# Four edits to a fused attention, gated-MLP and MLP kernel: load order, raw-word buffers, a PSUM bank, and the place of operand splits

## The chip, the cores and the metric

The kernel runs on one core of one Trainium2 chip. The metric is device time in microseconds (us); a measurement is the median of several executions. One execution was also profiled, and all rows below come from it.

## What is computed

Three layers in a row, all in float32, on 3072 tokens (4 sequences of 768) of width 512:

```python
# 1: chunked attention, 8 heads of 64; each chunk of 32 sees 16 keys left, 8 right, 8 memory keys
a = exp(scores - max(scores)); out = (a / sum(a)) @ v_full
# 2: RMS norm, then a gated MLP with 1536 hidden columns
xn = x / sqrt(mean(x * x) + 1e-6) * rms_g
x2 = silu(xn @ w_gate) * (xn @ w_val) @ w_out
# 3: a plain MLP with 2048 hidden columns
h = x2 @ w_in
g = where(h >= 1, h, where(h <= -1, 0, (h + 1) ** 2 / 4))
out = g @ w_out2
```

Weights arrive as float64 and are turned into float32 on the chip. Every product of two float32 matrices is made of three matmuls: each operand is split into a high part (rounded by a copy on ScalarE, ACT) and a low part (a subtraction on VectorE, DVE), and high*high, high*low and low*high are added up in PSUM (`mm3`, L555 to L559).

## The kernel before, in words

**Tiles and stages.** The tokens form six tiles of 512 (`NTT`). Before the first tile, a stretch written out by hand (`ORDER`, L25) runs the attention of the first four units (two units of heads make one pair of 128-row blocks). Then four tiles (t = 0 to 3) go one by one through the gated MLP: for each of 12 hidden blocks f, a gate product, a value product (`proj_in`, L561) and the output product of the block before (`out1`, L583). Each of these three is followed by a `slot` (L736), 36 slots in a tile. A slot holds a piece of the attention for later tiles (`att_slot`, by the tables `plan`, `plan2`, `plan3`) and a piece of weight conversion. The last two tiles go together through the gated MLP as a pair, and then all six tiles, as three pairs, through the last MLP, with a seven-product scheme for 2x2 block matrices (`seven`, L883): seven products of six matmuls instead of eight.

**Order of work.** In tile 0 the order on TensorE (PE) and on the queue of SyncE (SP), which issues most loads, is that of the program text (L674); the other engines are ordered by the compiler. From tile 1 on every engine works in the order of the text (L828). An instruction that must wait holds up all behind it on its engine or queue.

**Raw words.** In tile 0, each slot loads one 512 KB unit of raw float64 words of the gated MLP (`load_w`, L115, 36 units in all) into one of three buffers (`wst`, L72) and converts earlier units: `conv_c` (ACT, L128), `join` (DVE, L138 and L139, which is the last to read the buffer), then the high part (ACT, L152) and the low part (DVE, L154) in `wall`, which PE reads. Units 0 to 2 are loaded in the stretch `ORDER`, one more at each of d0 to d3. The tag `xn` of the pool `xs` holds `v_tail` in that stretch, and later the tile's normalised x; no one uses it in the first slots of tile 0.

**x.** A pair's normalised rows are transposed by PE in two blocks, x0 and x1, in successive slots (`step_x`, L533); four ACT copies take each out of PSUM (`part_X`, L546). Both use the first bank of the two-bank tile `ps_a`, which the attention steps use too. From tile 2 on, x goes to DRAM (L548) and comes back as a 1 MB load `load_x` (L552), which stands ahead of the gate product of f = 9. The next tile's split of x (`split_x`, L350) stands at f = 11. Loads of keys, queries and values (`load_qk`, L376; `load_v`, L392) are issued in the slot whose PE step frees their buffer; `load_v` for the unit after stands in the slot of a `v` step.

**Sevens and blocks ahead.** In `seven`, with five banks A to E, the products p0 to p6 go to A, C, B, A, B, C, B. After p0 and p1, ACT copies A into B (L891), on which p2 goes on adding, and C into `p5` (L892). DVE adds `p5` and B into C (L899) after p2; p4 writes B again, so p4 must wait for L899. After p4 DVE updates `p5` (L903). In the first pair's products `some` (L895) puts steps of weight conversion (`conv_step`) among the products. The hidden values h are used by `Out.run` (L992) in 7 G blocks, each needing a split operand `r`: `split` (L975) is an ACT copy (L982), a DVE subtraction (L984) and, for the first G blocks, a DVE sum written back into h (L986). `ahead(n)` makes the split of block n before the run begins. It stands right behind `proj1(f)` for odd f (L1122) and behind `proj2` for g = 3 to 6 (L1147), so its instructions lie on ACT and DVE ahead of the next seven's copies. `defer` (L893) is a list of calls that a seven makes right behind its two bank copies. At g = 6, the first step of the next pair's x (L812, a 1024-element DVE subtraction) is made behind the splits (L1154).

Of the kernel before, what the change touches and what calls it, by code (L numbers as in the profile page):

```python
# [39 lines left out]
def tile_stream_attention_moe_moe2(  # L40
# [69 lines left out]


    w1 = {}
    raw, absd, f32s = [], [], []

    def load_w(units, n):  # L115
        for _ in range(n):
            if units:
                dst, key, src = units.pop()
                w64 = wst.tile([P, 1024], U32, tag="w64", name="w64")
                nc.sync.dma_start(w64, src)  # L120
                raw.append((dst, key, w64))

# [402 lines left out]
            )  # L525

    def step_x(pr, blk, ps):
        t, o = divmod(pr, 2)
        if t == 1 and t not in xn_t:
            xn_t[t] = xs.tile([P, KK, TT], F32, tag="xn", name="xn")  # L530
        x = x_t[pr]
        for kk in range(KK):
            nc.tensor.transpose(ps[:, 0, kk * P:(kk + 1) * P], x[blk][:, kk * P:(kk + 1) * P], ident)  # L533
        ps_t["x", pr, blk] = ps

    def part_X(pr, blk):
        t, o = divmod(pr, 2)
        ps = ps_t.pop(("x", pr, blk))
        c0 = (2 * o + blk) * P
        if t < 2:  # L540
            xn = xn_t[t][:, :, c0:c0 + P]
        else:
            xn = x_t[pr][blk].rearrange("p (k i) -> p k i", k=KK)
        rows = ps[:, 0, :].rearrange("p (k i) -> p k i", k=KK)
        for kk in range(KK):
            nc.scalar.activation(xn[:, kk], rows[:, kk], AF.Copy, scale=g_t[:, kk:kk + 1])  # L546
        if t >= 2:
            nc.sync.dma_start(x_d[t][:, :, c0:c0 + P], xn)  # L548

    def load_x(t):  # L550
        xn_t[t] = xs.tile([P, KK, TT], F32, tag="xn", name="xn")
        nc.sync.dma_start(xn_t[t], x_d[t])  # L552
# [65 lines left out]
    for st in ORDER.split():  # L618
        c, n = st[0], st[1:]
        if c == "f":  # L620
            fill(slots[free[0]], int(n))
            continue
        n = int(n)
        if c in "savx":
            use[c, n] = free.pop(0)
            ps = slots[use[c, n]]
            if c == "x":
                step_x(n // 2, n % 2, ps)
            else:
                fns[c](n, ps)  # L630
                if n >= 4:
                    done.add(st)
            if c == "s" and n >= 3:
                load_qk(n + 1)
            if c == "v" and n >= 3:
                load_v(n + 1)
            if st == "s0":
                load_qk(3)
                load_v(2)
                load_v(3)  # L640
                load_w(units1, 1)
                nc.sync.dma_start(g_b, rms_g.partition_broadcast(P))
                nc.sync.dma_start(g_t, rms_g.rearrange("(k p) -> p k", p=P))
                load_w(units1, 2)
        elif c == "H":
            if not xhl:
                xh, xl = (xs.tile([P, KK, TT], F32R, tag=tag, name=tag) for tag in ("xh", "xl"))
                xhl.extend((xh[:, kk], xl[:, kk]) for kk in range(KK))
            nc.scalar.activation(xh[:, :, n * P:n * P + P], rows(n), AF.Copy)
        elif c == "L":  # L650
            dst, hi = (x[:, :, n * P:n * P + P] for x in (xl, xh))
            tt_(out=dst, in0=rows(n), in1=hi.bitcast(F32), op=ALU.subtract)  # L652
            free.append(use.pop(("x", n)))
        elif c == "r":
            step_r(n // 2, (n % 2,))
        elif c == "p":
            part_p(n)
        elif c == "c":
            conv_c()
        elif c == "d":  # L660
            conv_d()
            load_w(units1, 1)
        elif c == "g":
            lows.append(conv_hi())
        elif c == "o":
            lows.pop(0)()
        else:
            fns[c](n)
            if c in "mAn":
                free.append(use.pop(({"m": "s", "A": "a", "n": "v"}[c], n)))  # L670
# [31 lines left out]
    def att_step(pr, st):  # L702
        n = int(st[1])
        if st[0] in "sav" and f"{st[0]}{2 * pr + n}" in done:
            return
        if st[0] == "x":
            step_x(pr, n, ps_a)
            part_X(pr, n)
        elif st[0] == "r":
            step_r(pr)  # L710
        else:
            u = 2 * pr + n
            fns[st[0]](u, ps_a)
            for p in parts[st[0]]:
                fn = (lambda p=p: fns[p](u)) if p != "p" else (lambda: part_p(pr) if n else None)
                if pr < 4 or p in "mAn":
                    fn()
                else:
                    (later if p in "kp" else after).append(fn)
        if st[0] == "s":  # L720
            load_qk(2 * pr + n + 1)
        if st[0] == "v":
            load_v(2 * pr + n + 1)
# [101 lines left out]
    for t in range(NS):  # L825
        if t == 1:
            region.close()
            region.enter_context(tc.manual_schedule())  # L828
        for f in range(F1):
            if 0 < t < NS - 1 and f == 9:  # L830
                load_x(t + 1)
            if t == NS - 1 and f == F1 - 1:
                for i in range(8):
                    load_wp(i)
            proj_in(ps_g[0], w1[("g", f)])
            s = sp.tile([P, TT], F32, tag="s", name="s")
            nc.scalar.activation(s, ps_g[0], AF.Silu)
            if t == NS - 1 and f == 8:
                xq.extend(x_steps())
            slot(t, 3 * f)  # L840
            if t == NS - 1 and f == 6:
                att_only.close()
                right = ctx.enter_context(tc.tile_pool(name="right", bufs=1, side="right", reuse_waits="tile"))
                m2["y"] = right.tile([P, 2, KK, TT], F32, name="y")
                load_y(x_d[NS], x_d[NS + 1])
            proj_in(ps_g[1], w1[("v", f)])
            if f == F1 - 1 and t + 1 < NS:
                split_x(xn_t.pop(t + 1))
            nc.vector.tensor_tensor(out=s, in0=s, in1=ps_g[1], op=ALU.mult)
            low = split_h(f, s)  # L850
            if t == 0:
                low()
            slot(t, 3 * f + 1)
            if t:
                low()
            if pend is not None:
                out1(*pend)
            pend = (t, f)
            slot(t, 3 * f + 2)
# [18 lines left out]
        m2["n"] += 1  # L878
        return m2["t"][m2["n"] % len(m2["t"])]

    banks, defer = [], []

    def seven(n, early):  # L883

        A, B, C, D, E = banks
        banks[:] = D, A, E, C, B
        tt = nc.vector.tensor_tensor
        product(7 * n, A, True)
        product(7 * n + 1, C, True)
        p5 = tmp2("p5")  # L890
        nc.scalar.activation(B, A, AF.Copy)  # L891
        nc.scalar.activation(p5, C, AF.Copy)  # L892
        while defer:  # L893
            defer.pop(0)()
        some = lambda k: conv_step(PACE2[n // 4] * k) if n < F1 else None  # L895
        product(7 * n + 2, B, False)
        some(2)
        product(7 * n + 3, A, False)
        tt(out=C, in0=p5, in1=B, op=ALU.add)  # L899
        done11 = early(A)  # L900
        some(2)
        product(7 * n + 4, B, False)
        tt(out=p5, in0=p5, in1=B, op=ALU.add)  # L903
        some(2)
        product(7 * n + 5, C, False)
        some(1)
        product(7 * n + 6, B, False)
        return done11, C, B, p5
# [42 lines left out]
    class Out:  # L951
# [40 lines left out]
        def run(self, A, B, C, extra):  # L992
# [46 lines left out]
            while self.xq:  # L1039
                self.xq.pop(0)()  # L1040

    def done1(j, o, bank, p5):

        for m in range(2):
            d = p5[m] if p5 else tmp2("c")
            if p5:
                tt_(out=d, in0=p5[m], in1=bank[m], op=ALU.add)
            elif (j, o, m) == (1, 0, 1):
                nc.vector.tensor_copy(d, bank[m])
            else:  # L1050
                nc.scalar.activation(d, bank[m], AF.Copy)
            nc.scalar.dma_start(y_d[NS + o][:, 2 * j + m], d)
# [66 lines left out]
    for f in range(F1):  # L1119
        proj1(f)  # L1120
        if f % 2:
            o1.ahead(f // 2 - 1)  # L1122
        if f == 3:
            for i in range(4):
                load_wo(i)
        if f == 5:
            load_y(y_d[0], y_d[1])
            xq.extend(x_steps())
# [13 lines left out]
    for pr in range(NP2):  # L1142
        banks[:] = b3, Y[3], b4, b1, b2
        o2 = Out(G2, n1 + n2 * pr, 4, done2, xq)
        for g in range(G2):
            proj2(G2 * pr + g)
            o2.ahead(g - 3)  # L1147
            if pr and g < 2:
                defer.append(turn(pr - 1, 1, 0, g, Y[g]))
            if g == 3 and pr + 1 < NP2:  # L1150
                load_y(y_d[2 * pr + 2], y_d[2 * pr + 3])
                xq.extend(x_steps())
            if g == 6 and xq:
                xq.pop(0)()  # L1154
        extra = [
            (5 * G2 + 2, lambda: turns(pr, 0, 0)),
            (5 * G2 + 6, lambda: turns(pr, 1, 1)),
# [91 lines left out]
```

## Time and profile before

| what | us |
|---|---|
| three runs: median (lowest, highest) | 1159.44 (1158.72, 1161.72) |
| profiled execution, whole | 1158.09 |
| its span, first to last instruction | 1156.3 |
| busy: PE, DVE, ACT | 1125.6, 820.6, 617.3 |
| mean share of TensorE's clock granted | 0.989 |

The stretches of the span: attention alone until 36 us, tile 0 until 146, tiles 1 to 3 until 504 (tile 2 begins at 272), the first pair's 12 sevens of `proj1` until 619 and its output run until 671; then three times 8 sevens of `proj2` (the first until 755) and an output run, until 1152.

How to read it: PE is busy almost throughout, so the time between the matmuls, and any stretch at a lower clock, is what an edit can change. A row's idle time in square brackets is the engine's wait before that instruction, with what ended it; waits under 0.15 us are not shown there.

### The profile page before, as it was taken

What the parts mean: (1) busy time and instruction counts of PE and PEld (TensorE: products, weight loads), DVE (VectorE), ACT (ScalarE), POOL (GpSimd) and SP (SyncE); (2) the same over time, 40 slices, a digit from 0 to 9 for tenths busy, and PEclk for the clock granted to TensorE, in tenths of its full rate; (3) what the DMA queues carried; (4) which work ended last, traced back from release to release, by engine and by line L of the source; (5) the groups of instructions that cost most, each with busy time, mean ns of one, the idle gap of its engine ahead of it and who ended that gap; (6) DMA issues with size and microseconds to landing.
All of it is one profiled execution on the core that took longest, in us unless ns stands there. A gap on an engine that the chain in (4) does not pass through costs nothing.

```text
span 1156.3 us, 20945 instructions
## 1 busy us (share of the span) xinstructions
PE 1125.6 (97%) x7879; PEld 909.7 (79%) x7879; DVE 820.6 (71%) x1433; ACT 617.3 (53%) x1088; POOL 102.6 (9%) x152
## 2 busy tenths in 40 slices
PE   5899999999999999999999999999999999999998
PEld 4677788877788777887888888788887788887886
DVE  3887667767756666766676867897677887578855
ACT  3777665656565765534444634456444465344553
POOL 0200003213222222101110000000000000000000
PEclk7999999999999999999999999999999999999999
DMA  8776448998979887779997697756778666762564
GB/s 294 253 258 203 163 140 271 312 310 284 303 245 309 269 273 236 275 269 383 404 394 241 213 316 246 210 180 199 231 207 260 177 195 216 217 197 86 164 188 158
DMA packets 144212, 281.81 MB, mean 244 GB/s; under 512 B 15216, under 2 KB 65392, under 8 KB 142320
## 3 DMA queue, kind: packets, MB, share of 16 engines
q1 hardware_dynamic: 123664, 228.57, 60.7%
q0 software_dynamic: 12768, 43.52, 10.8%
q10 hardware_dynamic: 7680, 8.39, 2.1%
q8 instruction: 62, 1.02, 0.3%
q14 instruction: 38, 0.31, 0.1%
HBM read 201.26 MB, written 79.17 MB: 243 GB/s over the span
## 4 chain that ended last, share of the span: by engine, by line
PE 76%; DVE 8%; ACT 6%; DMA 6%; issue 3%; POOL 1%; SPq 0%; DVEq 0%; ACTq 0%; POOLq 0%
PE ps_y L1034 14%; PE ps_g L1034 11%; PE ps_g L557 6%; PE ps_g L559 5%; PE ps_g L558 5%; PE ps_g L872 3%; PE ps_b L872 3%; PE ps_b L874 3%; PE ps_b L873 3%; PE ps_g L874 3%; PE ps_g L873 3%; DMA w<-in_w_dram 3%; PE ps_y L557 3%; PE ps_y L558 3%; PE ps_y L559 3%
## 5 line engine op out<-in xcount | busy, mean ns | idle before, releaser
L557 PE MATMUL ps_g<-xh,wall 128*128 128x512 f32 x384 | 156.6, 408 | 3.2 <-ACT wall L152 3.2
L1034 PE MATMUL ps_y<-r,wo 128*128 128x512 f32 x672 | 156.2, 390 | 0.0
L558 PE MATMUL ps_g<-xl,wall 128*128 128x512 f32 x384 | 151.1, 394 | 0.4 <-DVE xl L652 0.4
L559 PE MATMUL ps_g<-xh,wall 128*128 128x512 f32 x384 | 151.3, 394 | 0.2 <-DVE wall L154 0.2
L1034 PEld LDWEIGHTS ps_y<-r,wo 128*128 128x128 f32 x672 | 125.7, 188 | 26.0
L984 DVE TENSOR_TENSOR r<-h,r 128x512 fp32r<-128x512 f32 x167 | 112.2, 689 | 44.0 <-ACT r L982 43.9
L935 ACT ACTIVATE t<-t,half 128x512 f32<-128x512 f32 x96 | 66.9, 720 | 128.4 <-DVE t L934 125.5
L982 ACT ACTIVATE r<-h 128x512 fp32r<-128x512 f32 x167 | 100.4, 624 | 56.2 <-DVE r L984 18.2
L1034 PE MATMUL ps_g<-r,wo 128*128 128x512 f32 x498 | 116.0, 390 | 0.0
L1034 PEld LDWEIGHTS ps_g<-r,wo 128*128 128x128 f32 x498 | 93.2, 188 | 19.4 <-DVE r L984 0.2
L557 PEld LDWEIGHTS ps_g<-xh,wall 128*128 128x128 f32 x384 | 72.8, 190 | 19.6 <-ACT wall L152 3.8
L559 PEld LDWEIGHTS ps_g<-xh,wall 128*128 128x128 f32 x384 | 72.7, 189 | 17.1 <-DVE wall L154 1.0
L558 PEld LDWEIGHTS ps_g<-xl,wall 128*128 128x128 f32 x384 | 73.0, 190 | 14.3 <-DVE xl L652 0.7
L872 PE MATMUL ps_g<-wall 128*128 128x512 f32 x198 | 78.4, 396 | 1.6 <-DVE ps_y L899 0.8
L872 PE MATMUL ps_b<-wall 128*128 128x512 f32 x202 | 79.2, 392 | 0.7 <-DVE ps_g L899 0.3
L873 PE MATMUL ps_b<-wall 128*128 128x512 f32 x202 | 78.6, 389 | 0.0
L874 PE MATMUL ps_b<-wall 128*128 128x512 f32 x202 | 78.6, 389 | 0.0
L557 PE MATMUL ps_y<-hh,wall 128*128 128x512 f32 x192 | 77.9, 406 | 0.0
L873 PE MATMUL ps_g<-wall 128*128 128x512 f32 x198 | 77.1, 390 | 0.0
L874 PE MATMUL ps_g<-wall 128*128 128x512 f32 x198 | 77.1, 389 | 0.0
L558 PE MATMUL ps_y<-hl,wall 128*128 128x512 f32 x192 | 75.2, 392 | 0.0
L559 PE MATMUL ps_y<-hh,wall 128*128 128x512 f32 x192 | 74.9, 390 | 0.0
(199 smaller groups left out, 2086.7 us busy)
## 6 DMA issues: line engine op xcount, KB each, us to landing
wo<-w2o_d SPq DMA_DIRECT2D x88, 512.0 KB, 3.4
wall<-w2p_d SPq DMA_DIRECT2D x168, 256.0 KB, 2.9
wall<-w1p_d SPq DMA_DIRECT2D x84, 256.0 KB, 5.9
w<-in_w_dram SPq DMA_DIRECT2D x36, 512.0 KB, 4.6
w<-in_w_dram POOLq DMA_DIRECT2D x32, 512.0 KB, 5.7
k_in<-in_k_dram SPq DMA_DIRECT2D x48, 256.0 KB, 4.9
wo<-w1o_d SPq DMA_DIRECT2D x21, 512.0 KB, 3.5
v_in<-in_v_dram SPq DMA_DIRECT2D x40, 260.0 KB, 4.3
```

The lines of the kernel that those rows point to most:

```text
L557: nc.tensor.matmul(ps, wh, xh, start=start, stop=False)
L558: nc.tensor.matmul(ps, wh, xl, start=False, stop=False)
L559: nc.tensor.matmul(ps, wl, xh, start=False, stop=stop)
L872: nc.tensor.matmul(bank, wh, xh, start=st, stop=False, skip_group_check=True)
L873: nc.tensor.matmul(bank, wh, xl, start=False, stop=False, skip_group_check=True)
L874: nc.tensor.matmul(bank, wl, xh, start=False, stop=kk == 1, skip_group_check=True)
L935: nc.scalar.activation(s, s, AF.Square, scale=0.5, bias=half)
L982: nc.scalar.activation(r[:, 0], src, AF.Copy)
L984: tt_(out=r[:, 1], in0=src, in1=r[:, 0].bitcast(F32), op=ALU.subtract)
L1034: nc.tensor.matmul(bank[p][m], a, b, start=s0, stop=s1, skip_group_check=True)
```

## The change

It moves `load_x` behind the slot of f = 9, and so behind what that slot issues. It gives two more raw-word buffers to units 3, 4, 8, 9, 13 and 14, in the memory of the tag `xn`, and loads two units at d0, so that every later unit is popped a slot earlier. It puts x1's transposes in the second bank of `ps_a`. It moves each split ahead of a run, but for the last, into the list `defer`, and the x step of g = 6 into a list `defer2`, which a seven calls behind L899 and the first use of A.

```diff
     def load_w(units, n):
...
                 dst, key, src = units.pop()
-                w64 = wst.tile([P, 1024], U32, tag="w64", name="w64")
+                i = 3 * F1 - 1 - len(units)
+                if i == 3:
+                    spare.append(xs.tile([P, 2, 1024], U32, tag="xn", name="w64s"))
+                if i < 15 and i % 5 > 2:
+                    w64 = spare[0][:, i % 5 - 3]
+                else:
+                    w64 = wst.tile([P, 1024], U32, tag="w64", name="w64")
...
     def step_x(pr, blk, ps):
-            nc.tensor.transpose(ps[:, 0, kk * P:(kk + 1) * P], x[blk][:, kk * P:(kk + 1) * P], ident)
+            nc.tensor.transpose(ps[:, kk * P:(kk + 1) * P], x[blk][:, kk * P:(kk + 1) * P], ident)
...
-        rows = ps[:, 0, :].rearrange("p (k i) -> p k i", k=KK)
+        rows = ps.rearrange("p (k i) -> p k i", k=KK)
...
-                step_x(n // 2, n % 2, ps)
+                step_x(n // 2, n % 2, ps[:, 0])
...
             conv_d()
-            load_w(units1, 1)
+            load_w(units1, 1 if n else 2)
...
-            step_x(pr, n, ps_a)
+            step_x(pr, n, ps_a[:, n])
...
-            if 0 < t < NS - 1 and f == 9:
-                load_x(t + 1)
...
             slot(t, 3 * f)
+            if 0 < t < NS - 1 and f == 9:
+                load_x(t + 1)
...
         done11 = early(A)
+        while defer2:
+            defer2.pop(0)()
         some(2)
...
+    def ahead(o, n, last):
+        if last:
+            o.ahead(n)
+        else:
+            defer.append(lambda: o.ahead(n))
...
         if f % 2:
-            o1.ahead(f // 2 - 1)
+            ahead(o1, f // 2 - 1, f == F1 - 1)
...
-            o2.ahead(g - 3)
+            ahead(o2, g - 3, g == G2 - 1)
...
             if g == 6 and xq:
-                xq.pop(0)()
+                defer2.append(xq.pop(0))
```

## Rows read from the trace of the kernel before

**Rows 1.** The page, its first part: busy us, share, instructions.

```profile
PE 1125.6 (97%) x7879; PEld 909.7 (79%) x7879; DVE 820.6 (71%) x1433; ACT 617.3 (53%) x1088; POOL 102.6 (9%) x152
```

**Rows 2.** Stretches: length, busy PE, PEld, DVE, ACT, POOL, clock, DMA share, GB/s.

```profile
36.00:48.00 12.00, 10.07 (x44) 7.87 (x45) 10.16 (x19) 9.95 (x15) 4.11 (x6) 1.00 0.93 313
60.00:72.00 12.00, 12.00 (x109) 9.30 (x108) 9.66 (x17) 9.67 (x15) 0.00 (x0) 0.86 0.85 288
...
252.00:264.00 12.00, 10.15 (x97) 8.18 (x98) 6.42 (x17) 2.80 (x7) 3.23 (x4) 0.86 0.69 236
```

**Rows 3.** PE's waits, whole span: total us, times, longest.

```profile
PE ps_g L557 <- ACT wall L152: 3.2, 2, 1.6
PE ps_a L453 <- ACT wgv L197: 2.3, 1, 2.3
PE ps_a L453 <- ACT aT L443: 2.2, 4, 0.7
PE ps_a L533 <- ACT x_nat L546: 1.8, 4, 0.6
```

**Rows 4.** Chain that ended last, in tile 0: start, us, what.

```profile
50.29 0.70 DVE tu L139
...
51.06 5.11 DMA w<-in_w_dram
```

**Rows 5.** The same chain in tile 1, around x's load.

```profile
244.96 1.13 SPq L552
...
246.99 7.16 DMA v_in<-in_v_dram
```

**Rows 6.** Timeline of PE in tile 1: start, duration, instruction, idle before.

```profile
253.67 0.35 PE L453 MATMUL ps_a<-v_in,aT 64*32 64x65 f32 x16 [2.35 <-ACT wgv L197]
```

**Rows 7.** Waits of PE's weight loads, 620 to 1157 us.

```profile
PEld ps_g L872 <- ACT ps_g L891: 3.3, 6, 0.5
```

**Rows 8.** Timeline of PE, `proj2`: p1 and p2 for g = 6, p4 for g = 7.

```profile
735.66 0.39 PE L872 MATMUL ps_g<-wall 128*128 128x512 f32 x1
...
737.30 0.50 PE L872 MATMUL ps_b<-wall 128*128 128x512 f32 x1
...
750.62 0.50 PE L872 MATMUL ps_g<-wall 128*128 128x512 f32 x1 [0.38 <-DVE ps_y L899]
```

**Rows 9.** Timeline of ACT in the seven of g = 6.

```profile
736.67 0.58 ACT L891 ACTIVATE ps_b<-ps_g 128x512 f32<-128x512 f32 x1
737.27 0.60 ACT L892 ACTIVATE t<-ps_g 128x512 f32<-128x512 f32 x1
```

**Rows 10.** Timeline of DVE in the sevens of g = 6 and g = 7.

```profile
737.48 0.69 DVE L984 TENSOR_TENSOR r<-h,r 128x512 fp32r<-128x512 f32 x1
738.20 0.69 DVE L986 TENSOR_TENSOR h<-h 128x512 f32<-128x512 f32 x1
739.06 0.70 DVE L899 TENSOR_TENSOR ps_g<-t,ps_b 128x512 f32<-128x512 f32 x1 [0.17 <-PE ps_b L874]
...
748.74 1.22 DVE L812 TENSOR_TENSOR y<-y 128x1024 f32<-128x1024 f32 x1
```

**Rows 11.** Timeline of ACT in the seven of f = 4, `proj1`.

```profile
544.85 0.60 ACT L892 ACTIVATE t<-ps_b 128x512 f32<-128x512 f32 x1 [0.72 <-PE ps_b L874]
```

**Rows 12.** Timeline of DVE in that seven.

```profile
545.39 0.42 DVE L190 TENSOR_TENSOR late<-tu 128x256 f32<-128x256 f32 x1
...
546.06 0.42 DVE L193 TENSOR_TENSOR late<-late,tu 128x256 f32<-128x256 f32 x1
...
546.86 0.69 DVE L899 TENSOR_TENSOR ps_b<-t,ps_y 128x512 f32<-128x512 f32 x1
```

**Rows 13.** Timeline of PE in that seven: the first matmuls of p2, p3, p4.

```profile
544.65 0.39 PE L872 MATMUL ps_y<-wall 128*128 128x512 f32 x1
...
546.01 0.39 PE L872 MATMUL ps_g<-wall 128*128 128x512 f32 x1
...
547.60 0.50 PE L872 MATMUL ps_y<-wall 128*128 128x512 f32 x1
```

More of the change, by code (lines that the diff above doesn't have):

```diff
@@ L112, in tile_stream_attention_moe_moe2 @@
     w1 = {}
-    raw, absd, f32s = [], [], []
+    raw, absd, f32s, spare = [], [], [], []
     def load_w(units, n):
@@ L879, in tmp2 @@
         return m2["t"][m2["n"] % len(m2["t"])]
-    banks, defer = [], []
+    banks, defer, defer2 = [], [], []
     def seven(n, early):
```

## The prediction

> **What bounds the kernel now.** Read the page's busy times first: PE is busy for 97% of the span [rows 1]. So an edit can pay only where PE waits or where its clock is down, and it costs only where it makes PE wait anew. Next come the list of PE's waits [rows 3] and the stretches with a clock under 1.00 [rows 2]; there the reader is to see four places. (1) In tile 0 the value products wait twice for converted weights, 1.6 us each, and the stretch behind the second wait has a mean clock of 0.86. Over 12 us that is 1.7 us of work lost ((1 - 0.86) x 12), which is 3.4 us at the lower level, 1.2 GHz, instead of 2.4. (2) In tile 1 a value step of the attention waits 2.35 us [rows 6], again with 0.86 behind it. (3) x1's transposes wait four times for x0's copies. (4) The weight loads of PE wait for the bank copy L891: six times on one bank [rows 7], three times each on two others, so 12, which are g = 4 to 7 of the three pairs. Last come the timelines of one seven of `proj2` and one of `proj1` [rows 8 to 13], where the reader is to see which instruction stands before which.
>
> Two prices recur. A product of six matmuls takes 1.36 us (p2 to p3, 544.65 to 546.01) [rows 13], 0.23 a matmul; a matmul's row lasts 0.39, so a wait costs PE about 0.16 more than the idle time it shows. And the first matmul behind a wait lasts 0.50 instead of 0.39, another 0.11.
>
> **x load behind attention's loads.** SP issued x's load at 244.96 and the second half of the next unit's values at 246.99; the latter landed 7.16 us later, at 254.15 [rows 5], while PE stood ready at 251.3 (253.67 less 2.35) [rows 6]. Behind the slot, x's 1 MB no longer lies ahead of the values: at the 313 GB/s of a full stretch [rows 2] that is 3.3 us, so they land at about 250.8. PE gets back 2.35 + 0.16 + 1.7 for the clock; I leave 0.2 for a landing that is not quite in time: **-4.0** (bounds -2.4 and -4.4). x's own load now stands on SP also behind the slot's stores of converted sums (L202), which wait for DVE, but x is read two blocks f later; in tile 2 the slot has no value load to free, and the move costs nothing for the same reason. What would uncover it is x landing behind f = 11. The Trainium skill, "DMA: Bandwidth & Descriptors", section "Queues, rings and completion order", says that each DMA engine takes turns between the queue rows that have work, packet by packet. If GpSimd's queue had work all that time, the values' half megabyte would go at half speed and land some 1.7 us later, and this part would be worth about 2.5 less; the one landing here can't tell.
>
> **Two more raw-word buffers.** On the chain in tile 0 a load goes out when a join frees its buffer (50.29) and takes 5.11 us [rows 4]; ACT's conversions wait for it, and PE for them. With five buffers units 3 and 4 go out at once behind `v_tail`'s last reader, and each unit to 14 is two joins ahead. Beyond that a load waits for the same join as before, but stands ahead of the key loads of the slot behind it. No wait for words then remains in slots 0 to 12. Of the first wait (1.6 + 0.16) about 0.65 stays, since its conversion chain on ACT and DVE is only held up by about 1.1; the second goes (1.75), and with it the 1.7 of clock [rows 2]. Three of the four waits for `aT` [rows 3] lie in tile 0, 1.5 us; there ACT's conversion, waiting for words, stood ahead of `aT`'s copy; with 0.16 each that is 2.0, of which I take 1.7. Together **-6.2** (bounds -1.5, if ACT and DVE themselves are the limit, and -7.2). Key loads wait up to a slot longer behind `load_w`; they are needed six slots later.
>
> **x's second block in the other bank.** x1 no longer waits for the four copies of x0, and the next unit's transposes into the first bank wait for x0's alone. 1.8 idle, four times 0.16, and some 0.1 for waits too short for the list: **-2.5** (bounds -2.9, and 0 if the wait were kept for the tile as a whole).
>
> **Blocks ahead behind bank copies, `proj2`.** Gone is L982 ahead of L891. p1 starts at 735.66 and p2 at 737.30 [rows 8], 0.28 more than 1.36, and 0.13 more is lost behind it: 0.41 x 12 = 4.9. Gone too, for the two pairs with a next x, is L812 ahead of L899 at g = 7 [rows 10]: 0.38 + 0.16 + 0.11 [rows 8], twice, 1.3. What is late next is p4, which writes the bank that L899 reads. L899 stands behind L984 and L986, which now stand behind L982, and that behind L892. L892 starts 0.20 after p2 (544.85, 544.65) [rows 11, 13], as it reads p1. The next ACT copy starts 0.60 after [rows 9] and ends 0.60 later; L984 starts then, L986 0.72 later [rows 10], L899 some 0.6 later and takes 0.70: 0.20 + 0.60 + 0.60 + 0.72 + 0.60 + 0.70 = 3.42, and PE goes 0.05 later, 3.47 after p2 instead of 2.72. (Behind L899 on DVE stands work on p3's and p4's results, and behind L982 on ACT the same, so nothing else is late with them.) I take 0.73 (0.69 to 0.80) and 0.11 for the restart: 0.84 x 12 = 10.1. Net 10.1 - 4.9 - 1.3 = **+3.9** (+2.6 to +5).
>
> **The same, `proj1`.** Four of its blocks move, into the sevens of f = 4, 6, 8, 10. There p2 never waited for L891, so nothing is won at p2. At p4, f = 4 and 10 lost 0.23 (547.60 less 546.01 less 1.36) [rows 13] and 0.11, together 0.7. But here the conversion's sums stand between the block and L899: L190 to L899 is 1.47 us, and in f = 6 and 8, where only two of the four stand there, L193 to L899, 0.80 [rows 12]. p4 comes late by 0.73 + 1.47 = 2.20 twice and 0.73 + 0.80 = 1.53 twice, each with 0.11: 7.9. Net **+7.2** (+5.5 to +8).
>
> **Clock.** A p4 that is 2.2 late leaves PE idle for 2.0 in the records. In tile 0 the clock stayed at 1.00 behind the first 1.6 us of idle time and fell behind the second; in tile 1 it fell behind 2.35 [rows 2, 3]. So each of the two long ones may cost 1.7. I take one: **+1.7** (0 to 3.4).
>
> **Sum.** -4.0 - 6.2 - 2.5 + 3.9 + 7.2 + 1.7 = **+0.1 us**. It is made against the profiled execution, 1158.09, which is 1.35 below the median of the three, 1159.44; the change is put on the median: 1159.5. About 0.3%, 3.5 us, is what a measurement can tell from no change.
>
> **Rivals.** *Faster: the blocks cost nothing where they now stand.* This needs L899 to be done in time all the same, by L984 and L986 finding room elsewhere. Then `proj2` wins 6.2 and `proj1` 0.7, no clock falls, and the sum is -12.7 - 6.9 = -19.6: 1139.8. Against it: L899 behind a ready L812 held PE up at g = 7 [rows 8, 10], so DVE keeps its order. 0.08. *Faster: the favourable ends.* Loads, values and bank at -7.2, -4.4, -2.9, p4 late by 0.69 and no fall of the clock: -14.5 + 9.8 = -4.7, 1154.7. 0.16. *Slower: the words were not the limit in tile 0.* DVE and ACT are busy for 10.16 and 9.95 of 12 us there [rows 2]. If the joins come no earlier with the words, PE keeps both waits and the fall: -1.5 in place of -6.2, the sum +4.8, 1164.3. It decides from where tile 0 gives back less than 2.8 us. For it: the engines' shares; against it: the load on the chain [rows 4]. 0.20. *An edit that does nothing:* x1's wait stays, as the tile is one to its readers; +2.6, 1162.0, inside no change. Part of the forecast's 0.56, as are no fall (-1.6) and two (+1.8).
>
> **Numbers.** Faster 0.08 + 0.16 = 0.24; the same 0.56; slower 0.20. The range runs from the favourable ends to tile 0's rival, 1154.0 to 1164.5; the first rival and a few hundredths on each side are left out.
>
> **What would show it.** Right: no wait of L453 in tile 1; none of L533; one wait of under 1 us for `wall`; no wait of PE's weight loads for L891; 16 waits of p4 for L899, 12 of about 0.55 idle, two of about 1.4, two of about 2.0; in each of those sevens L984 and L986 directly ahead of L899 on DVE. The forecast is wrong if p4 doesn't wait (the first rival), or if tile 0's second wait is there still.

## The result, and the profile after

The changed kernel takes 1166.62 us, the median of 5 executions (1164.83 to 1168.37), against 1159.44 of 5 of the kernel before (1157.73 to 1161.72) in the same comparison: a ratio of 1.0063, with a 95% interval of 1.0045 to 1.008. It is slower, by 7.2 us. The profiled execution has a span of 1164.5 against 1156.3, so the traces differ by 8.2.

Lines of the new file stand a few lines lower: what was L533 is L540, L546 is L553, L552 is L559, L872 is L879, L891 and L892 are L898 and L899, L899 is L906, L982, L984 and L986 are L991, L993 and L995.

First, the page's busy times after.

```profile
PE 1125.2 (97%) x7879; PEld 908.8 (78%) x7879; DVE 819.1 (70%) x1433; ACT 617.5 (53%) x1088; POOL 102.9 (9%) x152
```

Work is the same on every engine [rows 1]; what grew is the time between the matmuls. The best view for where is a list of marks: the start of each tile's and each seven's first ACT instruction, read from both timelines. The difference of a mark, after less before, runs like this:

| stage | difference at its end | gained or lost in it | forecast |
|---|---|---|---|
| start and tile 0 | -3.3 | -3.3 | -6.2 and a share of -2.5 |
| tile 1 | -5.4 | -2.1 | -4.0 and a share of -2.5 |
| tiles 2 and 3 | -5.0 | +0.4 | the rest of -2.5 |
| `proj1`, with its output run | +3.8 | +8.8 | +7.2 and +1.7 |
| `proj2`, three times, to the end | +8.2 | +4.4 | +3.9 |

The two lower lines came as forecast. Of the gains ahead of them, 12.7 in the sum, 5.0 are there. Next, PE's waits after (total us, times, longest).

```profile
PE ps_y L879 <- DVE ps_b L906: 3.8, 4, 2.0
...
PE ps_b L879 <- DVE ps_g L906: 3.5, 5, 1.3
PE ps_g L879 <- DVE ps_y L906: 3.2, 4, 1.3
...
PE ps_a L459 <- ACT aT L449: 3.0, 3, 1.2
PE ps_a L540 <- ACT x_nat L553: 2.5, 4, 1.3
PE ps_g L879 <- DVE ps_b L906: 2.0, 1, 2.0
PE ps_g L879 <- DVE ps_g L906: 1.8, 3, 0.6
...
PE ps_g L566 <- DVE wall L160: 0.7, 1, 0.7
...
PE ps_g L564 <- ACT wall L158: 0.3, 1, 0.3
```

There are seventeen waits for L906, 14.3 us in all. Before there were three, 1.1 in all: one of 0.3, which is still there, and two of 0.38 for p4 of g = 7, one of them in [rows 8]. The two waits for `wall` of 3.2 in all [rows 3] are gone; two short ones, 1.0 in all, stand there. The four of x1 for x0's copies are still there and longer, and so are those for `aT` [rows 3].

**`proj2`.** Timeline of DVE, and of PE's p4, in a seven with a deferred split:

```profile
743.18 0.69 DVE L993 TENSOR_TENSOR r<-h,r 128x512 fp32r<-128x512 f32 x1 [0.86 <-ACT r L991]
743.90 0.69 DVE L995 TENSOR_TENSOR h<-h 128x512 f32<-128x512 f32 x1
744.51 0.69 DVE L906 TENSOR_TENSOR ps_g<-t,ps_b 128x512 f32<-128x512 f32 x1
...
745.26 0.50 PE L879 MATMUL ps_b<-wall 128*128 128x512 f32 x1 [0.61 <-DVE ps_g L906]
```

L906 is directly behind the two, as forecast. p4 starts 0.77 later than without a wait, and its first matmul lasts 0.50 instead of 0.39: 0.88 in each of 12 sevens.

**`proj1`.** The seven of f = 4: ACT, DVE, then p4.

```profile
539.86 0.60 ACT L899 ACTIVATE t<-ps_b 128x512 f32<-128x512 f32 x1 [0.72 <-PE ps_b L881]
540.36 0.62 ACT L991 ACTIVATE r<-h 128x512 fp32r<-128x512 f32 x1
...
541.01 0.69 DVE L993 TENSOR_TENSOR r<-h,r 128x512 fp32r<-128x512 f32 x1 [1.85 <-ACT r L991]
541.74 0.69 DVE L995 TENSOR_TENSOR h<-h 128x512 f32<-128x512 f32 x1
542.35 0.42 DVE L196 TENSOR_TENSOR late<-tu 128x256 f32<-128x256 f32 x1
...
543.47 0.42 DVE L200 TENSOR_TENSOR late<-tu,late 128x256 f32<-128x256 f32 x1
543.81 0.69 DVE L906 TENSOR_TENSOR ps_b<-t,ps_y 128x512 f32<-128x512 f32 x1
...
544.56 0.50 PE L879 MATMUL ps_y<-wall 128*128 128x512 f32 x1 [2.02 <-DVE ps_b L906]
```

p4 is 2.18 late here and 2.17 at f = 10, and 1.50 at f = 6 and 8 (forecast 2.20 and 1.53). Stretches behind the first and the last of these waits (length, busy times, clock, DMA share, GB/s):

```profile
540.00:552.00 12.00, 9.98 (x45) 7.93 (x44) 7.87 (x15) 5.09 (x10) 1.26 (x2) 1.00 1.04 409
606.00:618.00 12.00, 10.72 (x40) 8.71 (x41) 5.51 (x10) 3.04 (x5) 1.42 (x2) 0.86 0.72 210
```

The clock fell behind one of the two long waits, f = 10, and not behind f = 4: 1.7 us, as taken. Nothing in these rows tells the two waits apart, so that it was one is luck.

**x1.** ACT's four copies of x0 and the transposes of x1, in tile 2:

```profile
268.52 1.12 ACT L553 ACTIVATE x_nat<-ps_a,g_t 128x128 f32<-128x128 f32 x4
...
269.70 0.66 PE L540 MATMUL ps_a<-ident,x_nat 128*128 128x128 f32 x4 [1.29 <-ACT x_nat L553]
```

x1 starts 0.06 behind the end of x0's last copy (269.64), although it goes to another bank.

**Tile 1.** The wait for values is down to 0.23 idle (0.44 in all), and the clock is 1.00 throughout. SP's issues, and what came later on DVE, ACT and PE:

```profile
241.72 2.31 SPq L398 DMA_DIRECT2D v_in<-in_v_dram  x2
244.08 1.95 SPq L559 DMA_DIRECT2D xn<-x_d  x1
246.12 0.39 SPq L208 DMA_DIRECT2D w1p_d<-wgv  x1
...
248.53 0.68 PE L459 MATMUL ps_a<-v_in,aT 64*32 64x65 f32 x45 [0.23 <-DMA v_in<-in_v_dram]
...
255.83 1.29 DVE L237 TENSOR_TENSOR wgv<-wall 128x512 f32<-128x512 f32 x2 [1.55 <-DMA w1p_d<-wgv]
...
259.50 0.63 ACT L203 ACTIVATE wgv<-s 128x512 fp32r<-128x512 f32 x1 [5.84 <-DVE s L200]
...
264.21 1.13 ACT L356 ACTIVATE xh<-xn 128x512 fp32r<-128x512 f32 x2
...
264.88 0.50 PE L564 MATMUL ps_g<-xh,wall 128*128 128x512 f32 x1 [0.30 <-ACT xh L356]
```

The reader is to see a chain from top to bottom. The stores of sums L208 go out behind x's 1 MB, as they did before, but PE and DVE come here some 5 us sooner. One of them frees `wgv` 1.55 after DVE wanted it. So DVE's sums are late, and so is ACT's copy L203, with what stands behind it: the split of x (L356) and x0's copies. PE waits 0.55 and 0.50 for the split, and x1's wait above is 1.45 instead of 0.72.

**Tile 0.** ACT and PE where `aT` is late:

```profile
66.30 1.28 ACT L842 ACT_TABLE_LOAD   x1
67.60 0.60 ACT L842 ACTIVATE s<-ps_g 128x512 f32<-128x512 f32 x1
68.09 0.59 ACT L449 ACTIVATE aT<-ps_a 128x512 f32<-128x512 f32 x1
...
68.74 0.46 PE L459 MATMUL ps_a<-v_in,aT 64*32 64x65 f32 x32 [1.08 <-ACT aT L449]
...
123.30 0.66 ACT L134 ACTIVATE tu<-w 128x512 f32<-128x512 f32 x1 [1.82 <-DMA w<-in_w_dram]
...
126.41 0.40 PE L459 MATMUL ps_a<-v_in,aT 64*32 64x65 f32 x23 [1.21 <-ACT aT L449]
```

At 68.1 `aT`'s copy stands behind a silu, and that behind a table load and three conversions that ACT made one behind the other from 64.57 on; the words of the last of them had landed 3 us before. At 125.8 it stands behind the same silu and table load, and these behind a conversion that did wait for its word.

### The profile page after: what moved, and what is told of

Its sections match the earlier page's. It is cut to its first block, busy times and chain, and to the rows that moved or that the text cites. A ratio compares the mean times of both kernels' runs of the same rounds, so it can differ in the third digit from the quotient of the medians.

```text
span 1164.5 us, 20927 instructions
## 1 busy us (share of the span) xinstructions
PE 1125.2 (97%) x7879; PEld 908.8 (78%) x7879; DVE 819.1 (70%) x1433; ACT 617.5 (53%) x1088; POOL 102.9 (9%) x152
## 4 chain that ended last, share of the span: by engine, by line
PE 81%; DVE 6%; ACT 5%; DMA 5%; issue 2%; SPq 0%; POOL 0%; ACTq 0%; DVEq 0%; POOLq 0%
PE ps_y L1043 14%; PE ps_g L1043 11%; PE ps_g L564 6%; PE ps_g L566 6%; PE ps_g L565 6%; PE ps_b L879 4%; PE ps_g L879 4%; PE ps_b L881 3%; PE ps_b L880 3%; PE ps_g L881 3%; PE ps_g L880 3%; PE ps_y L564 3%; PE ps_y L565 3%; PE ps_y L566 3%; DMA w<-in_w_dram 2%
## 5 line engine op out<-in xcount | busy, mean ns | idle before, releaser
L993 DVE TENSOR_TENSOR r<-h,r 128x512 fp32r<-128x512 f32 x167 | 112.2, 688 | 61.8 <-ACT r L991 61.8
L991 ACT ACTIVATE r<-h 128x512 fp32r<-128x512 f32 x167 | 100.7, 625 | 56.2 <-DVE r L993 17.5
L879 PE MATMUL ps_g<-wall 128*128 128x512 f32 x198 | 78.5, 397 | 7.0 <-DVE ps_y L906 3.2
L879 PE MATMUL ps_b<-wall 128*128 128x512 f32 x202 | 79.8, 395 | 3.5 <-DVE ps_g L906 3.5
```

The lines of the kernel that those rows point to most:

```text
L879: nc.tensor.matmul(bank, wh, xh, start=st, stop=False, skip_group_check=True)
L991: nc.scalar.activation(r[:, 0], src, AF.Copy)
L993: tt_(out=r[:, 1], in0=src, in1=r[:, 0].bitcast(F32), op=ALU.subtract)
```

## The experiments

Ratios are to the kernel before, measured on the same chip beside each group (medians 1160.12 for e1 to e4, 1160.32 for e5 to e12, 1161.52 for e13 to e16). The one traced execution of the kernel before took 1158.09, 2.0 to 3.4 less than these medians, so a gain read from two traces tends to be smaller than the one by medians.

**e1_splits_back: the changed kernel without the deferral.**

```diff
-            ahead(o1, f // 2 - 1, f == F1 - 1)
+            o1.ahead(f // 2 - 1)
...
-            ahead(o2, g - 3, g == G2 - 1)
+            o2.ahead(g - 3)
...
-                defer2.append(xq.pop(0))
+                xq.pop(0)()
```

> The changed kernel with its other three edits, but with the splits and the x step where they stood before. The theory: by the traces' stage marks the splits behind the bank copies cost 8.8 us in proj1 and 4.4 in proj2, all of it p4 waiting for L899 and one fall of the clock; so without them 1166.6 - 13.2 = 1153.4, no wait of p4 over 0.5, and PE's weight loads wait for the bank copy of A again. The rival: a part of that loss comes from the stages being reached 5 us earlier, with the conversion's steps in another phase, and stays without the deferral; then 1157 to 1160, with p4 waits left in proj1.

Measured: 1153.47, ratio 0.9948 (0.993 to 0.9965). That is 13.15 less than the changed kernel by the medians, and 13.8 if each is taken against the kernel before that was measured beside it. Between 500 us and the end PE waits for L905 (its L899) three times, 1.0 us in all, and its weight loads wait for the bank copy again, exactly as before [rows 7]:

```profile
PEld ps_g L878 <- ACT ps_g L897: 3.3, 6, 0.5
```

So the deferral is worth +13.2 to +13.8, forecast as 3.9 + 7.2 + 1.7 = 12.8. The rival falls: the stages are still reached early, and nothing is lost in them.

**e2_words and e3_xload: one edit alone on the kernel before.** e2 has the hunks of `load_w` and of `conv_d()`, e3 the two of `load_x`.

> The kernel before with the two raw-word buffers alone. The theory: the words come up to 11 us earlier, but ACT and DVE then set the pace of tile 0 and the waits for aT stay or grow, so tile 0 gives back 3.3 as in the changed kernel: 1159.4 - 3.3 = 1156.1, with at least two waits of over 0.5 for aT. The rival (the forecast's term): words were the limit, and what is missing was lost to another of the edits: -6.2, 1153.2, with no wait for aT.

Measured: 1155.55, ratio 0.9971 (0.9949 to 0.9993), 4.6 less, with bounds from 0.8 to 5.9. The timing lies between the two theories. The profiled execution gains 2.2 until the end of tile 0, and its waits there are:

```profile
PE ps_a L459 <- ACT aT L449: 2.0, 2, 1.1
PE ps_a L443 <- ACT e L438: 1.3, 2, 0.9
```

Two waits for `aT` and two for e stand where the forecast had none; on that the rival falls.

> The kernel before with x's load behind the slot alone. The theory: the wait for values and the clock's fall behind it go (4.2), but PE then comes too early for ACT's split of x at f = 11 and for x0's copies, and waits there about 2 more: -2.1, 1157.3. The rival (the forecast's term): nothing else is late, -4.0, 1155.4.

Measured: 1155.42, ratio 0.9954 (0.994 to 0.9969), 4.7 less (3.6 to 7.0). By the time the rival is right, although this run's trace shows the chain of the changed kernel. What goes with the gain is how long x's load takes. That changes from execution to execution: the changed kernel and e1 have the same code up to the end of tile 3, and they have the longest and the shortest load of this table:

| trace | x's load, us | DVE waits for `wgv` | gained in tile 1 |
|---|---|---|---|
| changed kernel | 9.6 | 1.55 | 2.1 |
| e3_xload | 9.4 | 1.62 | 2.6 |
| e13_words_xload (below) | 8.6 | 0.16 | 4.3 |
| e1_splits_back | 8.4 | none over 0.15 | 4.1 |

**e4_bank: the other bank alone.**

> The kernel before with x1's transposes in the second bank of ps_a alone. The theory: x1 still starts right behind x0's last ACT copy, since the two banks count as one buffer: no change of the span (within 0.5), and the four waits of x1 for x_nat stay, 1.8 in all. The rival (the forecast's term): the waits go, -2.5.

Measured (one execution): a span of 1157.5; over tiles 2 and 3, where most of these waits lie, the marks move by 0.1, and x1's waits are the same [rows 3]:

```profile
PE ps_a L533 <- ACT x_nat L546: 1.7, 4, 0.6
```

So the waits stay, and with them the cause of the forecast's gain; one execution can't tell a small difference of the time.

**e5_x_together: x1 issued ahead of x0's copies.**

```diff
-            step_x(pr, n, ps_a)
+            for b in range(2 - 2 * n):
+                step_x(pr, b, ps_a[:, b])
             part_X(pr, n)
```

> The kernel before with x1 in the second bank and its transposes issued right behind x0's, ahead of x0's ACT copies (x1's own copies stay in their slot). The theory: what x1 waited for was x0's copies, by the order in which the two uses of one buffer are issued; issued ahead of them it waits no more: PE's waits for x_nat fall from 1.8 to under 0.5, and the span by up to 2.5, to 1157.6. The rival: x1's wait is for its own rows (the ACT scaling of the second block), or the next attention step waits for the later copies instead; then a wait of the same size stands there, and the time stays at 1160.

Measured: 1158.53, ratio 0.9983 (0.9968 to 0.9998). PE's waits between 150 and 500 us:

```profile
...
PE ps_a L533 <- DVE e L423: 1.0, 1, 1.0
PE ps_a L407 <- ACT aT L443: 0.8, 1, 0.8
PE ps_a L437 <- ACT x_nat L546: 0.4, 1, 0.4
```

Not one x1 waits for x0 any more, with the same banks as in e4: what x1 waited for was x0's copies by the order of issue on one buffer, and not the bank. But 2.2 of waits stand in other places: x0 behind e, the next attention steps behind `aT` and x's copies. Cause by the first theory, price mostly by the rival.

**e8_mid1: the splits behind L899.**

```diff
         tt(out=C, in0=p5, in1=B, op=ALU.add)
+        while mid:
+            mid.pop(0)()
         done11 = early(A)
...
-            o2.ahead(g - 3)
+            ahead(o2, g - 3, g == G2 - 1, mid)
```

The same in `proj1`, and the x step of g = 6 behind the update of `p5`.

> The kernel before with the splits moved behind L899 (their ACT copy then stands behind both bank copies, their DVE part behind L899 and ahead of the first use of A), in proj1 and proj2, and the x step of g = 6 behind the update of p5 in the next seven. The theory: what cost 13 us was only the place ahead of L899 on DVE; here neither p2 nor p4 waits, so proj2 gives back 4.9 + 1.3 and proj1 0.7: -6.9, 1153.2. The rival: DVE is the bound of these sevens whatever the order, so that p6 waits for the update of p5, or the next seven's p0 for a bank, by what p2 no longer waits: 1160, or slower.

Measured: 1156.32, ratio 0.9967 (0.9951 to 0.9983), 4.0 less. DVE in the seven of g = 6:

```profile
739.06 0.70 DVE L899 TENSOR_TENSOR ps_g<-t,ps_b 128x512 f32<-128x512 f32 x1 [0.98 <-PE ps_b L874]
739.67 0.68 DVE L990 TENSOR_TENSOR r<-h,r 128x512 fp32r<-128x512 f32 x1
740.39 0.69 DVE L992 TENSOR_TENSOR h<-h 128x512 f32<-128x512 f32 x1
741.00 0.68 DVE L940 TENSOR_SCALAR t<-ps_g 128x512 f32<-128x512 f32 x1
...
740.17 0.39 PE L872 MATMUL ps_b<-wall 128*128 128x512 f32 x1
```

p4 goes at 740.17, without a wait, and p2 as well: the sevens of g = 4 to 6 gain 0.3 to 0.5 each. So the place on DVE was all that cost. By the marks, a pair with a next x is 2.2 ahead where its output run begins, but 1.1 of it is lost again in the run, since its first blocks wait for their splits (PE's weight loads for `r`: 3.0, six times). There DVE is the bound, as the rival has it for all sevens.

**e9_aT and e12_pool_low: what limits tile 0 behind the words.** Both are e2 with one more edit.

```diff
-        nc.scalar.activation(aT.rearrange("p g i -> p (g i)"), ps[:, 0, :], AF.Copy)
+        if 4 <= u < 8:
+            nc.vector.tensor_copy(aT.rearrange("p g i -> p (g i)"), ps[:, 0, :])
+        else:
+            nc.scalar.activation(aT.rearrange("p g i -> p (g i)"), ps[:, 0, :], AF.Copy)
```

> The kernel with the two raw-word buffers alone, and in tile 0 the copy of aT out of PSUM on DVE instead of ACT. The theory: behind the words the next limit of tile 0 is the order on ACT, where aT's copy stands behind a silu and its table load (1.29 + 0.6): on DVE the two waits for aT (1.1 and 0.9) go, and the time falls by about 2 against the buffers alone, 1155.6 to 1153.6. The rival: DVE is as full as ACT; the waits move to the converted weights or to e, and the time stays at 1155.6 or rises.

Measured: 1157.31, ratio 0.9961 (0.9942 to 0.998): by the ratios it can't be told from e2 (0.9971). In its trace the waits for `aT` fall from 2.0 to 0.3 and tile 0 ends 1.5 earlier than e2's, although x1 in tile 0 waits 1.2 for x0. Then tile 1 takes 2.2 more than in e2. Its wait for values is no longer (2.7 against e2's 2.9), but here the clock falls behind it. The stretch in e2, then in e9 (clock third from the end):

```profile
240.00:264.00 24.00, 20.83 (x239) 16.58 (x225) 17.01 (x38) 10.55 (x23) 5.09 (x7) 1.00 0.91 305
```

```profile
240.00:264.00 24.00, 21.21 (x203) 16.62 (x202) 15.18 (x34) 8.32 (x20) 3.96 (x5) 0.86 0.81 277
```

The cause of the `aT` waits was named rightly. Whether the gain would last in an execution whose clock stays up, e9 alone doesn't show.

```diff
-        return lambda: tt_(out=w[:, 1], in0=src, in1=w[:, 0].bitcast(F32), op=ALU.subtract)
+        eng = nc.gpsimd if len(units1) < 3 * F1 - 6 and key[1] % 2 else nc.vector
+        return lambda: eng.tensor_tensor(out=w[:, 1], in0=src, in1=w[:, 0].bitcast(F32), op=ALU.subtract)
```

> The kernel with the two raw-word buffers alone, and the low part of the converted weights of every other hidden block of tile 0 made on GpSimd, which is idle there, instead of DVE. The theory: DVE's and ACT's work is what tile 0 waits for, so 18 subtractions of 0.7 less on DVE shorten its waits for walls and e by 1 or more: a span of 1152.6 or less against 1153.65. The rival: DVE is not what the waits end on; no change, or longer if GpSimd's subtraction takes several us and PE waits for it.

Measured (one execution): a span of 1162.9, 9 more than e2's. A miss, but it tells little on tile 0's limit, since the work got slower, and the clock fell in tile 0 and in tile 1 (0.91 from 60 to 72, 0.86 from 252 to 264), which it did not in e2's trace. GpSimd's subtraction, and DVE's join beside it (ns min/median/max):

```profile
L161 POOL TENSOR_TENSOR wall<-tu,wall x18: 1287/1312/1923, 42.3 to 139.8; 128x512 fp32r<-128x512 f32 x18
...
L145 DVE SCALAR_TENSOR_TENSOR tu<-w,tu x54: 679/693/1699, 30.5 to 593.7; 128x512 uint32<-128x512 uint32 x54
```

**e13 to e16: the parts together.** e13 has words and x's load; e14 adds e5's edit; e15 adds e8's place for the splits and leaves the x step of g = 6 to the output run, which has a place for it; e16 adds e9's copy.

> The kernel before with the raw-word buffers and x's load behind the slot, x1 in the first bank. The theory: the bank edit does nothing, so this is the changed kernel without splits and bank, 1153.5 against 1160 of before, as the three together were. The rival: words (-4.6) and x's load (-4.7) add up in full, and the bank edit took 2.6 of it away: 1150.8.

> The same, with x1's transposes in the second bank and issued right behind x0's, ahead of x0's copies. The theory: the x1 waits, which the earlier PE makes longer (2.5 in the changed kernel), go: 2 less than the kernel without it, 1151.5. The rival: as in the trace of that edit alone, most of it comes back as waits of the next attention steps for e and aT: no difference, 1153.5.

Measured: 1154.34, ratio 0.9943 (0.9924 to 0.9962), and 1154.71, 0.9941 (0.992 to 0.9963). e13 lies beside e1 (0.9948), so no gain of the bank edit shows there either, though the intervals would hide one of some 2 us. e14 gains 1.1 in tiles 1 to 3 against e13's trace, but in its profiled execution, the slowest of its six, PE waits 6.1 for `aT` in tile 0 (e13: 2.5), and the clock falls behind the last of these waits (0.86 from 132 to 144). No difference by the medians: the rival.

> The same three edits, with the splits behind L899 in proj1 and proj2, and the x step of g = 6 left to the output run that follows. The theory: 0.39 for each of the 12 sevens of proj2 (4.7), 0.7 in proj1, and the stall of p4 at g = 7 (1.3) all come back, as nothing late is left on DVE at the run's start: 6.5 less than the three edits alone, 1145. The rival: DVE is late at the run's start anyway, so that the run's first blocks wait for their splits: 4 less, 1147.5.

> The same as the one before, with tile 0's copy of aT on DVE. The theory: tile 0 gives back the 1.5 that its trace showed, and no wait for values in tile 1 takes it away again: 1.5 less. The rival: the waits go over to e and x1 in tile 0: no difference.

Measured: 1149.74, ratio 0.99 (0.9885 to 0.9914), and 1147.33, 0.9883 (0.9866 to 0.9899). The splits in their new place give 5.0 on e14, between theory and rival; DVE's low parts `r` are still late at the run's start:

```profile
PE ps_y L1047 <- DVE r L997: 1.1, 4, 0.3
```

DVE's copy of `aT` brings 2.4 more by the medians, by intervals that overlap a little; in the traces the waits for `aT` in tile 0 are 3.9 in e15 and 0.3 in e16. e16 is 1.2% below the kernel before, and so beats both kernels.

## Why the prediction was wrong

The forecast of no change failed by 7.2 us, and the losses are not where it failed.

- **The deferral was right:** +13.2 to +13.8 measured by e1 against 12.8, and the 16 waits of p4 stand as forecast, 12 of 0.6, two of 1.3 and two of 2.0. In `proj2` 0.88 x 12 = 10.6 was paid where the forecast had 10.1; the gain at p2, by the marks, is 0.88 - 0.49 = 0.39 for each (forecast 0.41), and g = 7's stall went. In `proj1` p4 was late by 7.8 with its restarts, and one fall of the clock was added; that it was one of the two was luck.
- **The bank was wrong by its whole 2.5.** The step "x1 no longer waits for the four copies of x0" took the bank as the thing waited for. e4 and e5 show that it was the order in which two uses of one two-bank buffer are issued. The "edit that does nothing" among the rivals was the case, by the waits.
- **The raw words were over-estimated.** The second wait and its fall of the clock went as said (3.4). But the step that gave back 1.7 for `aT`, because ACT's conversion "waiting for words" stood ahead of its copy, was wrong: at 68.7 the words had landed, and ACT was at work without a pause from 64.57 on; at 126.4 a conversion did wait for a word, but for one that the two buffers don't serve (they end with unit 14). Tile 0's waits for `aT` and e went from 1.5 to 2.9 instead of to nothing. The stage gave 3.3 for 6.2; e2 alone 4.6, with an interval that takes in both. Engines as the limit, the slower rival, holds for `aT` and e, not for the two waits for weights; by its own sign, less than 2.8 given back in tile 0, it falls in three of four traces with the buffers (the changed kernel 3.3, e1 2.9, e13 3.3), and not in e2's (2.2).
- **Both falls of the clock that the gains took back, 1.7 each, were counted in full from one trace, and not every execution has them.** In tile 0 the clock stayed at 1.00 in e3 and e8, which leave tile 0 as it was, behind second waits of 1.5 and 1.7 (1.56 in the kernel before, where it fell). Yet these two reach tile 1 only 0.7 earlier and 0.4 later than the kernel before, and not 1.7 earlier: PE waits 2.8 and 4.4 there for `aT` and x0's copies, where the kernel before waits 1.5. So at least part of this term was not there to be won. For tile 1 the last section has the waits with a fall and without.
- **x's load was right in its mechanism and on the median** (4.7 alone, forecast 4.0); in the profiled execution it gave 2.1, because the step "x is read two blocks later" followed x alone, and the stores ahead of it on SP, and not the stores behind it, which hold `wgv`: the one that DVE waits for lands at 255.74, 0.5 earlier than before (256.21), while PE comes some 5 us sooner.
- The Trainium skill's "DMA: Bandwidth & Descriptors", section "Queues, rings and completion order", was cited for queues that take turns, by which the values could land 1.7 later. Between 241.7 and 248.5 GpSimd's queue took 20.5% of the engines' time and SP's 76.7%, and PE lost 0.44: that delay did not come, but the other queue was not full either, so the rule was not put to the test.

Taken together: the three gains measured 6.65 (e1) or 7.2 (e13) where 12.7 was forecast. 2.5 of what is missing is the bank, some 3 tile 0, where `aT` and e, and not the words, then hold PE up. Whether words and x's load hinder each other stays open: alone they sum to 9.3, but the intervals of e2 and e3 are as wide as the difference to 7.2.

## What to carry to other kernels

A split that must be made somewhere is free only if the engine's next deadline lies behind it: list for each queue what comes next and who waits for it, and put the work behind that, not merely behind what it delayed before. A wait is for what the program's order makes it wait for; before moving data to another bank, see whether issuing the consumer's work earlier takes the wait away. And a gain early in a chain of stages is kept only if no later stage holds a wait that absorbs it: of the 2.2 that a pair's sevens won in e8, 1.1 went again in the output run behind them.

## What the runs showed of the hardware

- **A low clock that cost nothing.** In the first 48 us the granted clock differed between executions, and the time did not. The stretch from 16 to 48 us in the kernel before (clock 0.74), then in e4_bank (1.00):

```profile
16.00:48.00 32.00, 24.00 (x448) 17.97 (x430) 23.35 (x49) 19.47 (x38) 5.51 (x8) 0.74 0.74 250
```

```profile
16.00:48.00 32.00, 23.69 (x415) 18.15 (x401) 22.00 (x46) 18.32 (x39) 5.21 (x7) 1.00 0.74 248
```

  The table load ahead of tile 0's first silu starts at 38.58 in the one and 38.60 in the other, so up to there the low clock cost no time.
- **The same idle time, and not the same clock.** After 2.02 us of idle time the clock stayed at 1.00 (544.56), after 2.01 us it fell (607.27), both in the changed kernel. With x's load in its old place PE waits for values in tile 1: the clock fell behind 2.35 (before), 3.38 (e5), 2.24 (e8), 2.67 (e9) and 2.08 us (e12), and stayed at 1.00 behind 2.94 (e2) and 2.21 us (e4).
- **Joins on DVE last longer beside GpSimd.** In e12 the 13 joins of DVE that overlap a subtraction of GpSimd last 1.29 us on average and up to 1.77, the other 55 last 0.69.
- **Table loads.** On ACT a change between exp and silu shows as a row of 1.28 us, with the next instruction 0.02 behind it (66.30, 67.60). The Trainium skill, "ScalarE: Activation LUTs", section "What ACT_TABLE_LOAD costs", adds a drain of 1.38 to the same 1.28, for 2.66 in all; here the instruction ahead ended at 66.29, so the trace shows 1.31, and the measurement decides.
- **Executions differ by more than one edit.** x's load took 7.3 to 9.6 us in five traces, and the kernel before ranged from 1156.35 to 1164.59 over 59 executions.
